# Attention, routing and two networks on one core: weight copies of the routing issued a round earlier, place matrices made on one engine

## The chip, the core and the metric

The kernel runs on one core of a Trainium2 chip. A core has a matrix engine (TensorE, PE in the rows; PEld is its loading of weights), a vector engine (VectorE, DVE), a scalar engine (ScalarE, ACT), a general engine (GpSimd, POOL) and a queue engine (SyncE, SP) that here does nothing but issue transfers (DMAs). Each engine works through its own list of instructions in order, and they wait for each other by semaphores. SBUF is the memory beside the engines, PSUM the one that TensorE writes its products to, and DRAM the large memory. The metric is the time of one execution on the device, in microseconds (us).

## What is computed

Windowed attention, then a mixture of 8 experts in which each token goes to one expert with room for 288 tokens each, then a gated network:

```python
def _moe_ref(x, w_gate, w1, w2):
    N, D = x.shape                      # 2304, 512
    E = w_gate.shape[1]                 # 8
    cap = N // E                        # 288
    logits = x @ w_gate
    order = np.argsort(-logits.flatten())
    ...
    for idx in order:                   # best (token, expert) pair first
        tok, e = (int(idx) // E, int(idx) % E)
        if assigned[tok] >= 0 or counts[e] >= cap:
            continue
        assigned[tok] = e
        counts[e] += 1
    ...
    for e in range(E):
        mask = assigned == e
        out[mask] = np.maximum(x[mask] @ w1[e], 0.0) @ w2[e]

def reference(**kwargs):
    attn_out = _attn_ref(...)           # 4 x 8 heads x 576 x 64, window 64
    x = attn_out.transpose(0, 2, 1, 3).reshape(2304, 512)
    x = _moe_ref(x, ...)
    return _moe2_ref(x, ...)            # silu(x @ w_gate) * (x @ w_val) @ w_out
```

## The kernel before

The program has four stages, one behind the other: attention (all heads, leaving the tokens transposed in `xT`), routing (which expert takes which token), the experts, and the gated network. The order of the instructions on each engine is the order in which the code is written; there is no scheduler.

**Routing.** `routing()` finds the assignment in six rounds of a parallel search, `step(it, ...)`. A round goes over the engines like this. DVE makes from the scores `M` and the shifted logits `U` each token's wish: `m`, `below`, `Us`, `u`, `G` (`wants()`). TensorE counts the wishes in 18 small matmuls (`cnt`). DVE compares the counts with the room (`sat`). TensorE spreads the result to all partitions (`low`, `tot`). ACT copies the count of ties (`ties`) and the new window (`cg`) from PSUM. DVE updates the scores (`lt`, `M`), and POOL narrows `U` with `cg` in four instructions (`narrow()`), which the next round's `Us` reads.

**Beside the routing.** Two other pieces of work are interleaved with the rounds.
- *Rows of tokens.* `store_rows(3)` takes three blocks of 128 tokens: TensorE transposes a block into PSUM (`rowps`, three buffers), ACT copies it to SBUF (`row`, six buffers), and SP stores it to DRAM (`xrows`, 256 KB each). Three blocks (rows 0 to 2) stand ahead of the first round, and three more behind each of the first five rounds (`beside`), 18 in all. The experts later gather their tokens from `xrows` by index, so the first gather waits for all 18 stores.
- *Weight tiles.* The experts' weights come as tiles of 128 x 1024 (512 KB) through four buffers `wraw`, and each is split into a coarse part `whi` and a remainder `wlo`, so that products keep float32 precision. `Stream.half()` does half a tile: ACT copies `whi` (L59), DVE subtracts `wlo` (L60). A round has one such half, between the count and `sat`, so that six rounds split three tiles. `half()` first calls `load()`, which issues the next tile's load on SP once a buffer is to be free: the fifth tile's load takes the first tile's buffer and waits for the `wlo` of its second half, in the second round; the sixth tile's waits for the fourth round, and the seventh's for the sixth.

**Places.** Behind the rounds `assign()` ranks the tokens of each expert, and `places()` makes from each token's place two matrices of zeros and ones, in two halves of nine blocks of tokens. `A` has the place's lower 6 bits. `T` has the upper bits, and `B` is `T` times the token's number, in two parts: part 0 times the block (`crow`), on POOL, and part 1 times the partition (`pcol`), on ACT. `indices()` multiplies `A` and `B` on TensorE (`ps_i`), and DVE adds up the indices (`idx`). Every engine then reads a flag that says whether the search has settled and branches around the slow path; the gathers (POOL, `gather()`) and the experts begin.

Of the kernel before, what the change touches and what calls it, by code (L numbers as in the profile page):

```python
# [12 lines left out]
OP = mybir.AluOpType  # L13
# [5 lines left out]
NT = NTOK // 128  # L19


class Stream:
# [24 lines left out]
    def half(self):  # L47

        if self.nsplit == len(self.todo):
            return  # L50
        self.load(self.nsplit + 5)
        key, _ = self.todo[self.nsplit]
        t = self.raws[self.nsplit]
        if key not in self.parts:
            self.parts[key] = [p.tile(list(t.shape), F32R, name=n) for p, n in ((self.hi, "whi"), (self.lo, "wlo"))]
        h, lo = self.parts[key]
        m = t.shape[1] // 2
        sl = (slice(None), slice(self.nhalf * m, self.nhalf * m + m))
        self.nc.scalar.activation(h[sl], t[sl], AF.Copy)  # L59
        self.nc.vector.tensor_tensor(lo[sl], t[sl], h[sl].bitcast(F32), op=OP.subtract)  # L60
        self.nhalf = 1 - self.nhalf
        self.nsplit += not self.nhalf
# [6 lines left out]
class Kernel:  # L69
# [381 lines left out]
    def build(self):  # L451
        nc, tc = self.nc, self.tc
        self.constants()
        self.weights_setup(self.ctx)

        self.big = self.pool("big", 1).tile([128, 4, NTOK], F32, name="big")
        self.xT = self.big[:, :, 0:NTOK]
        self.ffn_stream()
        with ExitStack() as ctx:
            self.attention(ctx)  # L460
        self.st.open(self.ctx, tc)
        self.xg_ctx = ExitStack()
        self.xg_p, self.xg = self.xg_ctx.enter_context(tc.tile_pool(name="xg", bufs=4, side="right")), {}
        with ExitStack() as ctx:
            self.rows_setup(ctx)
            self.store_rows(3)
            def beside(i):
                self.store_rows(3)
                self.convert_move()

            self.routing(ctx, beside)
        self.ffn()
# [111 lines left out]
    def routing(self, ctx, beside=lambda i: None):  # L584


        nc, L = self.nc, self.L
        mm = nc.tensor.matmul
        BIG = 1.0e30

        def pool(name, bufs, space=None):
            kw = {} if space is None else {"space": space}
            return ctx.enter_context(self.tc.tile_pool(name=name, bufs=bufs, **kw))

        rp, r1 = pool("rp", 2), pool("r1", 1)
        self.rps = pool("rps", 1, PS)
        full = [128, NT, NE]
        first, more = 6, 4
        oh = r1.tile(full, BF, name="oh")
        one = r1.tile([1, NE + first + more], F32, name="one")  # L600
        ties, flag = r1.tile([1, NE], F32, name="ties"), r1.tile([1, 1], I32, name="flag")

        halves = slice(0, 11), slice(11, NT)

        def step(it, M, U, sp, G=None):
            bl = self.below[it % 2]
            if G is None:
                G = rp.tile([128, NT, 32], BF, name="G")
                tmp = [rp.tile([128, NT], F32, name="m"), rp.tile(full, F32, name="Us"), rp.tile([128, NT], BF, name="u")]
                list(self.wants(M, U, bl, G, tmp, halves))  # L610
            cnt = self.rps.tile([32, NE + 1], F32, name="cnt")
            for c in range(NT):
                mm(cnt, G[:, c, :], bl[:, c, :], start=c == 0, stop=c == NT - 1)
            if it < first:
                self.st.half()
            nc.vector.tensor_scalar(self.sat[0:32], cnt[:, 0:NE], cnt[:, NE:NE + 1], 0.5 - CAP,
                                    op0=OP.subtract, op1=OP.is_le)
            nc.scalar.activation(ties, cnt[0:1, 0:NE], AF.Copy, accum_out=one[:, NE + it:NE + it + 1])
            low, ps = self.rps.tile([128, NE], F32, name="low"), self.rps.tile([128, 2, NE], F32, name="tot")
            mm(low, self.weights[0], self.sat, start=True, stop=True)  # L620
            for i in range(2):
                mm(ps[:, i, :], self.weights[i + 1], self.sat, start=True, stop=True)
            cg = sp.tile([128, 2, NE], F32, name="cg")
            nc.scalar.activation(cg, ps, AF.Copy)
            lt = rp.tile(full, F32, name="lt")
            M2 = sp.tile(full, F32, name="M")
            for s in halves:
                nc.vector.tensor_tensor(lt[:, s], U[:, s], low[:, None, :].to_broadcast([128, s.stop - s.start, NE]), op=OP.is_lt)
            for s in halves:
                nc.vector.scalar_tensor_tensor(M2[:, s], lt[:, s], -BIG, M[:, s], op0=OP.mult, op1=OP.add)  # L630
            return M2, cg

        def narrow(U, cg, sp):
            U2 = sp.tile(full, F32, name="U")
            for x, y, i, op in ((U2, U, 0, OP.subtract), (U2, U2, 1, OP.mult)):
                for s in halves:
                    nc.gpsimd.tensor_tensor(x[:, s], y[:, s], cg[:, None, i, :].to_broadcast([128, s.stop - s.start, NE]),
                                            op=op)
            return U2

        def assign(M, n):

            m = rp.tile([128, NT], F32, name="m")
            for s in halves:
                nc.vector.tensor_reduce(m[:, s], M[:, s], axis=AX.X, op=OP.max)
            for s in halves:
                nc.vector.tensor_tensor(oh[:, s], M[:, s], m[:, s, None].to_broadcast([128, s.stop - s.start, NE]), op=OP.is_ge)
            rank = self.ranks(rp, oh)
            tot = self.rps.tile([128, NE], F32, name="tot")
            for c in range(NT):  # L650
                mm(tot, self.onesb, oh[:, c, :], start=c == 0, stop=c == NT - 1)
            off = rp.tile([1, NE + n], F32, name="off")
            wrong = rp.tile([1, 2], F32, name="wrong")
            nc.scalar.activation(off[:, 0:NE], tot[0:1], AF.Square, bias=self.expect[:, 0:1], accum_out=wrong[:, 0:1])
            nc.scalar.activation(off[:, NE:], one[:, NE:NE + n], AF.Square, bias=self.expect[:, 1:2],
                                 accum_out=wrong[:, 1:2])
            self.places(rp, oh, rank)
            nc.vector.tensor_scalar(flag, wrong[:, 0:1], wrong[:, 1:2], 1.0e6, op0=OP.add, op1=OP.min)
            self.indices(rp)

        def unsettled():
            return nc.values_load(flag[0:1, 0:1], min_val=0, max_val=10 ** 6) > 0

        list(self.wants_first(12, NT))
        M, U = L, self.U
        for it in range(first):
            M, cg = step(it, M, U, rp, self.G if it == 0 else None)
            if it < first - 1:
                U = narrow(U, cg, rp)
            beside(it)  # L670
        self.store_rows(NT)
        assign(M, first)
        self.gather_first()
        with self.tc.If(unsettled()), ExitStack() as c1:  # L674
            rq = c1.enter_context(self.tc.tile_pool(name="rq", bufs=2))
            for it in range(first, first + more):
                U = narrow(U, cg, rq)
                M, cg = step(it, M, U, rq)
            assign(M, first + more)
            with self.tc.If(unsettled()), ExitStack() as c2:  # L680
                self.choose(c2, rp)
            self.gather_first()
# [22 lines left out]
    def places(self, rp, oh, rank):  # L705

        nc = self.nc
# [13 lines left out]
        self.B = rp.tile([128, NT, 2, 2 * NT], BF, name="B")  # L721
        T = rp.tile([128, NT, 2 * NT], F32, name="T")
        sq = [128, NT // 2, 2 * NT]
        for s in parts:
            nc.vector.tensor_tensor(T[:, s], self.half[:, None, :].to_broadcast(sq), pt[:, s, None].to_broadcast(sq),
                                    op=OP.is_equal)
        for s in parts:
            nc.gpsimd.tensor_tensor(self.B[:, s, 0, :], T[:, s], self.crow[:, s, None].to_broadcast(sq), op=OP.mult)
            nc.scalar.activation(self.B[:, s, 1, :], T[:, s], AF.Copy, scale=self.pcol)
        for s in parts:  # L730
            sh = [128, NT // 2, 64]
            nc.vector.tensor_tensor(self.A[:, s], self.row[:, None, 0:64].to_broadcast(sh),
                                    pp[:, s, None].to_broadcast(sh), op=OP.is_equal)

# [421 lines left out]
```

## Time and profile before

| | |
|---|---|
| time of the runs | 838.07 us median of 3 (836.49 to 838.79) |
| the profiled execution's own time | 837.96 us |
| its span in the trace | 836.2 us |
| TensorE | busy 803.2 us, 96% of the span |
| DVE | busy 516.7 us, 62% |
| ACT | busy 396.4 us, 47% |
| POOL | busy 95.4 us, 11% |

The span is from the first to the last instruction of the program; a little lies around it. Shares are means over stages with different limits, so a change in one stage is read from that stage. In a row of the timeline the first number is the start of the instruction, the second its duration (of several merged ones, from the first's start to the last's end); in brackets stands how long the engine had been idle and whose end it had waited for.

### The profile page before, as it was taken

How to read it: one execution, taken by the hardware profiler on the slowest of the kernel's cores; microseconds unless marked ns; L12 is line 12 of the kernel's file. 1: busy time of each engine (PE TensorE's matmuls, PEld its weight loads, DVE VectorE, ACT ScalarE, POOL GpSimd, SP SyncE). 2: the span in 40 equal slices, each digit the busy share in tenths (PEclk: the TensorE clock that was granted, in tenths of full speed). 3: DMA queues.
4: the chain of work that ended last, by engine and by line, in shares of the span. 5: the costliest groups of instructions: out<-in, count | busy, mean ns of one | idle time of the engine just before them, and what ended most of it. 6: DMA issues, size and time to landing. Idle time of an engine off the chain costs nothing.

```text
span 836.2 us, 14893 instructions
## 1 busy us (share of the span) xinstructions
PE 803.2 (96%) x5635; PEld 752.7 (90%) x5635; DVE 516.7 (62%) x1104; ACT 396.4 (47%) x998; POOL 95.4 (11%) x167
## 2 busy tenths in 40 slices
PE   8999986499999999999999999999999999999997
PEld 6888966399999999999999999999999999999996
DVE  6777868668888788898774443554453355344322
ACT  5989965346565666674332332333232243222211
POOL 6333323400010000000000000110000012000002
PEclk9999996699999999999999999999999999999999
DMA  8999916569798897777632211331211223220001
GB/s 182 189 192 189 282 49 216 172 192 289 273 294 268 275 287 260 243 265 265 203 115 73 76 51 51 111 116 51 76 51 51 75 89 114 76 67 10 1 1 75
DMA packets 92332, 123.72 MB, mean 148 GB/s; under 512 B 24416, under 2 KB 59232, under 8 KB 92256
## 3 DMA queue, kind: packets, MB, share of 16 engines
q1 hardware_dynamic: 89376, 113.28, 45.9%
q0 software_dynamic: 2880, 9.44, 3.3%
q8 instruction: 46, 0.75, 0.4%
q14 instruction: 30, 0.25, 0.1%
HBM read 99.63 MB, written 18.87 MB: 142 GB/s over the span
## 4 chain that ended last, share of the span: by engine, by line
PE 43%; issue 33%; DVE 2%; POOL 2%; DMA 0%; ACT 0%; POOLq 0%; DVEq 0%; ACTq 0%
PE psw L943 12%; PE psg L943 12%; PE psa L943 11%; PE pso L943 6%; POOL out_dram L1088 1%; PE psw L975 1%; DMA w<-t 0%; DVE wlo L60 0%; PE psw L437 0%; DVE sg L1060 0%; DVE t L896 0%; DVE t L900 0%; ACT xt L935 0%; DVE y L936 0%; POOLq L1152 0%
## 5 line engine op out<-in xcount | busy, mean ns | idle before, releaser
L943 PE MATMUL psg<-y,whi 128*128 128x384 f32 x1152 | 223.1, 336 | 0.0
L943 PEld LDWEIGHTS psg<-y,whi 128*128 128x128 f32 x1152 | 201.6, 188 | 0.0
L60 DVE TENSOR_TENSOR wlo<-wraw,whi 128x512 fp32r<-128x512 f32 x236 | 155.2, 687 | 9.9 <-ACT whi L59 5.2
L59 ACT ACTIVATE whi<-wraw 128x512 fp32r<-128x512 f32 x236 | 136.6, 622 | 2.9 <-ACTq L674 2.9
L1056 DVE TENSOR_TENSOR sg<-sg,psg 128x384 f32<-128x384 f32 x72 | 39.8, 553 | 156.4 <-ACT sg L1055 156.3
L943 PE MATMUL pso<-whi,p 128*128 128x512 f32 x432 | 133.3, 390 | 0.0
L943 PE MATMUL psg<-y,wlo 128*128 128x384 f32 x576 | 123.5, 336 | 0.7 <-DVE sg L1056 0.7
L1055 ACT ACTIVATE sg<-psg 128x384 f32<-128x384 f32 x72 | 35.3, 491 | 174.8 <-PE psg L943 174.8
L943 PEld LDWEIGHTS psg<-y,wlo 128*128 128x128 f32 x576 | 102.5, 188 | 3.8 <-DVE sg L1056 1.2
L1062 ACT ACTIVATE p<-sg 128x384 fp32r<-128x384 f32 x72 | 37.8, 525 | 120.4 <-DVE sg L1060 120.4
L943 PEld LDWEIGHTS pso<-whi,p 128*128 128x128 f32 x432 | 80.6, 188 | 14.5
L943 PE MATMUL pso<-wlo,p 128*128 128x512 f32 x216 | 84.2, 390 | 0.0
L943 PE MATMUL psw<-xt,whi 128*128 128x288 f32 x512 | 78.5, 296 | 0.0
L943 PE MATMUL psa<-hl,whi 128*128 128x288 f32 x256 | 75.6, 295 | 0.1
L943 PE MATMUL psa<-hh,whi 128*128 128x288 f32 x256 | 75.5, 295 | 0.0
L943 PE MATMUL psa<-hh,wlo 128*128 128x288 f32 x256 | 75.3, 294 | 0.0
L943 PEld LDWEIGHTS psw<-xt,whi 128*128 128x128 f32 x512 | 71.5, 188 | 0.0
L1088 POOL DMA_INDIRECT out_dram<-orow,idx x18 | 17.5, 972 | 456.9 <-ACT orow L1086 270.9
L1063 DVE TENSOR_TENSOR p<-sg,p 128x384 fp32r<-128x384 f32 x72 | 40.2, 558 | 42.6 <-ACT p L1062 42.6
L932 ACT ACTIVATE hh<-psw 128x288 fp32r<-128x288 f32 x64 | 26.3, 411 | 58.4 <-PE psw L943 58.4
L226 ACT ACTIVATE pp<-ps_s,nm 128x128 f32<-128x128 f32 x144 | 50.9, 365 | 5.1 <-DVE nm L219 4.5
L1060 DVE TENSOR_TENSOR sg<-sg,psg 128x384 f32<-128x384 f32 x72 | 39.8, 552 | 20.7 <-PE psg L943 20.7
(176 smaller groups left out, 1103.4 us busy)
## 6 DMA issues: line engine op xcount, KB each, us to landing
wraw<-in_moe_w_dram SPq DMA_DIRECT2D x64, 512.0 KB
wraw<-w SPq DMA_DIRECT2D x54, 512.0 KB
w<-t SPq DMA_DIRECT2D x36, 256.0 KB
raw<-in_moe_w_gate_dram SPq DMA_DIRECT2D x12, 512.0 KB
raw<-in_moe_w_val_dram SPq DMA_DIRECT2D x12, 512.0 KB
raw<-in_moe_w_out_dram SPq DMA_DIRECT2D x12, 512.0 KB
rawq<-in_q_dram SPq DMA_DIRECT2D x32, 144.0 KB
rawk<-in_k_dram SPq DMA_DIRECT2D x32, 144.0 KB
```

Source lines behind the costliest of these rows:

```text
L59: self.nc.scalar.activation(h[sl], t[sl], AF.Copy)
L60: self.nc.vector.tensor_tensor(lo[sl], t[sl], h[sl].bitcast(F32), op=OP.subtract)
L226: nc.scalar.activation(PP[g][:, u, :], ps[:, u, :], AF.Exp, bias=nm[:, u:u + 1], scale=scale, accum_out=SM[g][:, u:u + 1])
L932: nc.scalar.activation(h, x, AF.Relu)
L943: self.nc.tensor.matmul(acc, x, y, start=start and i == 0, stop=stop and i == len(seq) - 1)
L975: nc.tensor.transpose(ps[:, d, :], self.xg[t][r0:r1, 128 * d:128 * d + 128], self.ident[r0:r1, r0:r1])
L1055: nc.scalar.activation(sg, pg, AF.Sigmoid)
L1056: nc.vector.tensor_tensor(sg, sg, pg, op=OP.mult)
L1060: nc.vector.tensor_tensor(sg, sg, pv, op=OP.mult)
L1062: nc.scalar.activation(p[0][:, sl], sg, AF.Copy)
L1063: nc.vector.tensor_tensor(p[1][:, sl], sg, p[0][:, sl].bitcast(F32), op=OP.subtract)
L1088: d = nc.gpsimd.indirect_dma_start(out=self.out, out_offset=bass.IndirectOffsetOnAxis(ap=self.idx[:, 6 * g + t:6 * g + t + 1], axis=0), in ...
```

## The change

Two edits.

`half()` is cut in two: `high()` is the ACT copy with what stands ahead of it, the call of `load()` included, and `low()` the DVE subtraction. In the routing `low()` stays where `half()` was. `high()` moves ahead: the first one before the first three rows, and each further one behind `narrow()`, before the row copies of its round. Everywhere else `half()` calls both, one after the other, as before.

In `places()` DVE makes part 0 of `B` in place of POOL, and it does `T`, `B` and `A` of the first half before those of the second.

```diff
     def half(self):
         if self.nsplit == len(self.todo):
             return
+        self.high()
+        self.low()
+
+    def high(self):
         self.load(self.nsplit + 5)
         key, _ = self.todo[self.nsplit]
...
         self.nc.scalar.activation(h[sl], t[sl], AF.Copy)
+        self.next = h, lo, t, sl
+
+    def low(self):
+        h, lo, t, sl = self.next
         self.nc.vector.tensor_tensor(lo[sl], t[sl], h[sl].bitcast(F32), op=OP.subtract)
...
             self.rows_setup(ctx)
+            self.st.high()
             self.store_rows(3)
...
             if it < first:
-                self.st.half()
+                self.st.low()
...
             if it < first - 1:
                 U = narrow(U, cg, rp)
+                self.st.high()
             beside(it)
...
+        sh = [128, NT // 2, 64]
         for s in parts:
             nc.vector.tensor_tensor(T[:, s], self.half[:, None, :].to_broadcast(sq), pt[:, s, None].to_broadcast(sq),
                                     op=OP.is_equal)
-        for s in parts:
-            nc.gpsimd.tensor_tensor(self.B[:, s, 0, :], T[:, s], self.crow[:, s, None].to_broadcast(sq), op=OP.mult)
             nc.scalar.activation(self.B[:, s, 1, :], T[:, s], AF.Copy, scale=self.pcol)
-        for s in parts:
-            sh = [128, NT // 2, 64]
+            nc.vector.tensor_tensor(self.B[:, s, 0, :], T[:, s], self.crow[:, s, None].to_broadcast(sq), op=OP.mult)
             nc.vector.tensor_tensor(self.A[:, s], self.row[:, None, 0:64].to_broadcast(sh),
                                     pp[:, s, None].to_broadcast(sh), op=OP.is_equal)
```

The list of ACT from the last copy ahead of the routing (`lt`) to the second round's `cg`, before (an x3 merges three row copies):

```order
L286 ACTIVATE lt<-ps_l 128x512
L429 ACTIVATE row<-rowps 128x4x2x64 x3
L59 ACTIVATE whi<-wraw 128x512
L618 ACTIVATE ties,one<-cnt 1x8
L624 ACTIVATE cg<-tot 128x16
L429 ACTIVATE row<-rowps 128x4x2x64 x3
L59 ACTIVATE whi<-wraw 128x512
L618 ACTIVATE ties,one<-cnt 1x8
L624 ACTIVATE cg<-tot 128x16
```

The same piece with the change, whose lines are numbered eight or nine higher:

```order
L294 ACTIVATE lt<-ps_l 128x512
L63 ACTIVATE whi<-wraw 128x512
L437 ACTIVATE row<-rowps 128x4x2x64 x3
L627 ACTIVATE ties,one<-cnt 1x8
L633 ACTIVATE cg<-tot 128x16
L63 ACTIVATE whi<-wraw 128x512
L437 ACTIVATE row<-rowps 128x4x2x64 x3
L627 ACTIVATE ties,one<-cnt 1x8
L633 ACTIVATE cg<-tot 128x16
```

In each round `whi` and the three row copies have changed places; `ties` and `cg` stand behind both, as before.

The list of SP through the whole routing, before: stores of rows (`xrows`) and loads of weight tiles (`wraw`), up to the flag of the branch:

```order
L431 DMA xrows<-row 128x512 x3
L43 DMA wraw<-in_moe_w_dram 128x4x256
L431 DMA xrows<-row 128x512 x6
L43 DMA wraw<-in_moe_w_dram 128x2x512
L431 DMA xrows<-row 128x512 x6
L43 DMA wraw<-in_moe_w_dram 128x4x256
L431 DMA xrows<-row 128x512 x3
L662 TENSOR_LOAD flag
```

The same with the change:

```order
L43 DMA wraw<-in_moe_w_dram 128x4x256
L439 DMA xrows<-row 128x512 x6
L43 DMA wraw<-in_moe_w_dram 128x2x512
L439 DMA xrows<-row 128x512 x6
L43 DMA wraw<-in_moe_w_dram 128x4x256
L439 DMA xrows<-row 128x512 x6
L671 TENSOR_LOAD flag
```

Each of the three loads has moved ahead of three stores: 3, 6, 6 and 3 stores around them have become 0, 6, 6 and 6.

The list of DVE in `places()`, from the bits of the place (`pt`, `pp`) to the indices, before:

```order
L718 TENSOR_SCALAR pt<-pos 128x18
L719 TENSOR_SCALAR pp<-pos 128x18
L725 TENSOR_TENSOR T<-half,pt 128x324 x2
L732 TENSOR_TENSOR A<-row,pp 128x576 x2
L658 TENSOR_SCALAR flag<-wrong 1x1
L744 TENSOR_REDUCE idx<-ps_i 64x18 x2
```

With the change:

```order
L728 TENSOR_SCALAR pt<-pos 128x18
L729 TENSOR_SCALAR pp<-pos 128x18
L736 TENSOR_TENSOR T<-half,pt 128x324
L739 TENSOR_TENSOR B<-T,crow 128x9x36
L740 TENSOR_TENSOR A<-row,pp 128x576
L736 TENSOR_TENSOR T<-half,pt 128x324
L739 TENSOR_TENSOR B<-T,crow 128x9x36
L740 TENSOR_TENSOR A<-row,pp 128x576
L667 TENSOR_SCALAR flag<-wrong 1x1
L752 TENSOR_REDUCE idx<-ps_i 64x18 x2
```

DVE has two instructions more, and the order is by halves; POOL, whose list isn't shown, has two fewer.

## Rows read from the trace of the kernel before

**Rows 1.** Stretches: us, busy PE, PEld, DVE, ACT, POOL; PE clock, DMA share, GB/s

```profile
122.20:157.20 35.00, 21.03 (x245) 18.23 (x243) 27.95 (x112) 18.27 (x49) 8.59 (x23) 0.71 0.54 181
166.30:836.20 669.90, 662.92 (x4004) 633.73 (x4004) 395.31 (x694) 273.66 (x546) 31.46 (x49) 1.00 0.42 139
```

**Rows 2.** Waits, 122 to 157: total us, times, longest

```profile
DVE wlo L60 <- ACT whi L59: 3.3, 5, 0.9
```

**Rows 3.** Timeline of the third round: ACT and DVE

```profile
133.88 0.62 ACT L59 ACTIVATE whi<-wraw 128x512 fp32r<-128x512 f32 x1
...
134.53 0.69 DVE L60 TENSOR_TENSOR wlo<-wraw,whi 128x512 fp32r<-128x512 f32 x1 [0.92 <-ACT whi L59]
135.15 0.21 DVE L616 TENSOR_SCALAR sat<-cnt 32x8 bf16<-32x8 f32 x1
...
135.45 0.17 ACT L618 ACTIVATE ties<-cnt 1x8 f32<-1x8 f32 x1 [0.95 <-DVE sat L616]
...
135.72 0.18 ACT L624 ACTIVATE cg<-tot 128x16 f32<-128x16 f32 x1
```

**Rows 4.** Timeline of the SP queue in the routing

```profile
123.59 1.33 SPq L431 DMA_DIRECT2D xrows<-row  x3
130.22 0.38 SPq L43 DMA_DIRECT2D wraw<-in_moe_w_dram  x1
130.66 4.80 SPq L431 DMA_DIRECT2D xrows<-row  x6
139.45 0.38 SPq L43 DMA_DIRECT2D wraw<-in_moe_w_dram  x1
...
148.98 0.38 SPq L43 DMA_DIRECT2D wraw<-in_moe_w_dram  x1
```

**Rows 5.** Timeline of ACT: copies of rows 9 to 11, and of row 15

```profile
136.34 1.84 ACT L429 ACTIVATE row<-rowps 128x512 f32<-128x512 f32 x3 [0.43 <-DMA xrows<-row]
...
145.41 0.60 ACT L429 ACTIVATE row<-rowps 128x512 f32<-128x512 f32 x1 [0.81 <-PE rowps L427]
```

**Rows 6.** Stretches behind the loads, columns as in rows 1

```profile
131.00:134.20 3.20, 2.99 (x30) 2.58 (x29) 2.62 (x12) 2.00 (x4) 1.20 (x4) 0.61 0.86 236
...
152.00:154.00 2.00, 0.00 (x0) 0.00 (x0) 1.97 (x6) 1.56 (x6) 1.09 (x2) 0.50 1.07 401
...
155.00:156.00 1.00, 0.55 (x9) 0.40 (x8) 0.76 (x2) 0.00 (x0) 0.03 (x1) 0.50 0.00 0
```

**Rows 7.** Timeline from the fifth round's window to the sixth's split

```profile
144.42 0.18 ACT L624 ACTIVATE cg<-tot 128x16 f32<-128x16 f32 x1
...
145.92 0.48 DVE L570 SCALAR_TENSOR_TENSOR Us<-below,U 128x88 f32<-128x88 bf16 x2 [0.28 <-POOL U L637]
...
148.26 0.69 DVE L60 TENSOR_TENSOR wlo<-wraw,whi 128x512 fp32r<-128x512 f32 x1 [0.85 <-ACT whi L59]
```

**Rows 8.** Timeline of the place matrices on DVE and POOL

```profile
152.33 0.50 DVE L725 TENSOR_TENSOR T<-half,pt 128x324 f32<-128x324 int32 x1
...
152.91 0.92 POOL L728 TENSOR_TENSOR B<-T,crow 128x324 bf16<-128x324 f32 x1 [6.76 <-DVE T L725]
153.15 1.28 DVE L732 TENSOR_TENSOR A<-row,pp 128x576 bf16<-128x576 int32 x1
153.78 1.24 POOL L728 TENSOR_TENSOR B<-T,crow 128x324 bf16<-128x324 f32 x1
...
154.36 1.28 DVE L732 TENSOR_TENSOR A<-row,pp 128x576 bf16<-128x576 int32 x1
```

**Rows 9.** Timeline of first and third gather, TensorE's use, and the gathers' landing

```profile
157.17 1.22 POOL L443 DMA_INDIRECT xg<-xrows,idx  x1 [2.14 <-DVE idx L744]
...
159.94 0.95 POOL L443 DMA_INDIRECT xg<-xrows,idx  x1 [0.30 <-issue]
...
165.08 0.32 PEld L975 LDWEIGHTS psw<-ident,xg 32*128 32x128 f32 x4 [0.17 <-issue]
...
DMA to landing us min/median/max: 3.7/4.7/5.5
```

## Prediction

> **What bounds the kernel now.** I read the stretches first [rows 1]. From 166.30 us to the end of the span TensorE is busy for 662.92 of 669.90 us: the two networks are one stream of matmuls, and whatever moves their start moves the end one for one. In the 35 us of the routing (122.20 to 157.20) TensorE is busy for 21 us only, and VectorE (DVE) for 27.95. Nothing of the networks can start before the routing has its indices, so here a chain of small dependent steps sets the time. The change touches only this stretch.
>
> The waits of the stretch [rows 2] give one entry of the size that matters: DVE waits 3.3 us in 5 of the 6 rounds for `whi`, ScalarE's (ACT's) copy of half a weight tile. One round shows why [rows 3]. ACT reaches `whi` at 133.88 only, since three row copies stand ahead of it. DVE had nothing to do for 0.92 us, starts `wlo` at 134.53, and `sat`, with which the next part of the round begins, stands behind `wlo` on DVE (135.15). From `sat` the round goes on to `cg` on ACT (135.72), to POOL's new `U`, and over DVE's `Us`, `u` and `G` to the next count.
>
> Three times the SP queue stands in this chain's shadow [rows 4]: a load of a weight tile goes out at 130.22, 139.45 and 148.98, each right behind the `wlo` that frees its buffer (148.26 + 0.69 = 148.95 for the last [rows 7]), and everything behind that load on the queue waits with it.
>
> **The first part: the ACT copy a round earlier.** With `high()` in front of the row copies, `whi` is done long before DVE asks for it, in the first round too: ACT has it before its first row copy, where it waits for TensorE anyway. The 3.3 us of idle time [rows 2] go. Count and `sat` follow at once, since in the round shown the count is through before `wlo` is. **Term 1: -3.3 us.** The ACT copies are as many as before and DVE's `wlo` stays at its place.
>
> But `high()` also holds the call that issues the next load, and so the load moves ahead of three row stores on SP: before, stores 0 to 2 went out at 123.59, ahead of the load of 130.22 [rows 4]. Now they stand behind it, and the load waits for `wlo` of the second round. The row copies have six buffers: row 6 writes into the buffer of row 0, and cannot until store 0 has landed. In the new order that is a store queued behind a 512 KB load. The same comes back two rounds on: rows 12 to 14 need stores 6 to 8, which now stand behind the load that waits for the fourth round's `wlo`.
>
> How long from the issue of the load to the landing of the first store behind it (L)? One row shows it: row 9 waited for store 3, the first behind the load of 130.22, and started at 136.34 after 0.43 us of waiting [rows 5], so L = 136.34 - 130.22 = 6.1 us. The bytes alone give a lower end: load and one store are 0.79 MB, and from 131.00 to 134.20 the DMA engines moved 236 GB/s, 0.76 MB [rows 6], so they are through at about 134.3, L = 4.1. The second such batch has an upper end too: row 15, which needs the first store behind the load of 139.45, started at 145.41 with TensorE as its last wait [rows 5], so there L is at most 6.0. I take 6.1 for the first batch, as the row at the same place says, and the middle of 4.1 and 6.0, 5.0, for the second.
>
> The Trainium skill's page "DMA: Bandwidth & Descriptors" (Why a DMA increments its semaphore by 16 and not by 1) has the engines of one DMA finish independently, and only the last of them completes it; row 9's landing, later than the bytes, agrees. By that rule the slowest engine would count in both batches, 6.1 and 6.0, and the sum would be 1.0 us higher than mine.
>
> What a late landing costs, counted from the load's issue: `sat` of that round started 0.10 us before it (`sat` comes 0.62 after the start of `wlo` [rows 3], the load 0.72 after it [rows 4, 7]). A round without waiting takes 0.57 from `sat` to `cg` [rows 3]; then 2.99 from `cg` (144.42) to the time at which DVE would have started `wlo` (148.26 - 0.85 = 147.41 [rows 7]), in a round in which `Us` was already waiting for POOL's `U`, so that `cg` is what counts; then 0.62: 4.18 in all. Undisturbed, the `sat` two rounds on would come at -0.10 + 2 x 4.18 = 8.26. Disturbed, three row copies (1.84 us [rows 5]) start at L, and `ties` and `cg` of the next round stand behind them on ACT: `cg` at L + 1.84 + 0.27 [rows 3], and `sat` 3.61 later, at L + 5.72. Behind ACT wait POOL's `U`, then DVE's `Us` and `G`, and TensorE's next count; TensorE's transposes of the next rows wait for the same copies but have no use for the time. The cost is L + 5.72 - 8.26 = L - 2.54. **Term 2: +3.6 us** (L = 6.1; 1.6 at 4.1). **Term 3: +2.5 us** (L = 5.0; 1.6 to 3.5). Rows 9 to 11 and 15 to 17 wait for the stores just behind, and are reached later; I cost them at nothing.
>
> At the end six row stores instead of three stand behind the load of 148.98. With three, the DMA engines were idle from 155.00 on, 6.0 us after the load's issue [rows 6]; three more of 262 kB at 401 GB/s [rows 6] make it 8.0. The first gather, which reads all rows, came 8.19 after that load (157.17 [rows 9]). So this one is just hidden, and the gathers have 0.4 us to spare: the third goes out at 159.94 and lands 4.7 later, 164.6, and TensorE takes it up at 165.08 [rows 9]. **Term 4: 0**, up to +1.5 if the last store has a tail of 2 us as in row 9.
>
> **The second part: the place matrices.** Before, DVE makes both halves of T, then both of A, while POOL makes its half of B. A takes 1.28 us per half [rows 8], and both end 0.61 us after an instruction of POOL does: 153.15 + 1.28 = 154.43 against 152.91 + 0.92 = 153.83, and 155.64 against 155.02. So I read A as 0.6 us of work and 0.67 of being held up. Now T, B and A follow on DVE, twice: 0.50 + 0.50 (B has T's shape, its nearest row) + 0.61, twice 1.6, from 152.33 to about 155.5. Before, A ended at 155.64. **Term 5: -0.1 us.** Had A needed 1.28 us of itself, two times 2.28 would end at 156.9, 1.2 us later. ACT's half of B is covered by A in either.
>
> The Trainium skill's page "SBUF — State Buffer" (Who interferes with whom) says that a DVE instruction with two SBUF inputs is held up completely by a GpSimd instruction that reads SBUF. The two ends here agree, and by that rule the term is -0.1 and not +1.2.
>
> **The sum.** The profiled execution took 837.96 us (span 836.2, the rest lies around it), 0.1 below the median of the runs, 838.07. -3.3 + 3.6 + 2.5 + 0 - 0.1 = +2.7: 837.96 + 2.7 = 840.7. With every bound at its low end (L = 4.1 twice) it is -0.2, 837.8; at its high end (L = 6.1 and 6.0) +3.7, 841.7.
>
> **The rivals.**
> *The stores never hold the copies up* (the other side): only terms 1 and 5 stay, -3.4, 834.6. It needs stores 0 to 2 to land before ACT wants row 6, some 1.4 us after the load (`cg` at 0.47, the new `whi` of 0.62 and one step). Against it: no row shows a store landing less than 4 us after a load ahead of it. The point at which the change pays is a mean L of 4.2. Chance 0.07.
> *Landings as early as the bytes allow*: L near 4.1 in both, -0.2 to +1, about 838.4. For it: the 6.1 is one row. Chance 0.18.
> *The gathers become the last wait too*: term 4 at up to 1.5 on top of the forecast, 842.2. For it: the margin computed is 0.2 us. Chance 0.09.
> *A is slow by itself*: +1.3 on the forecast, 842.0; against it both ends of rows 8. Chance 0.04.
> *The forecast*, both stalls in place, +1.3 to +3.9: 0.62.
>
> **How the numbers follow.** 0.3% of 838 is 2.5 us, about what a measurement of this kernel can tell from no change. The forecast's case lies around that line: 0.36 above, 0.26 below. Faster: 0.07 and 0.01 of the second rival, 0.08. Same: 0.26 + 0.17 = 0.43. Slower: 0.36 + 0.09 + 0.04 = 0.49. The range leaves out the first rival and the upper part of the last two: 837.7 to 842.4. For the forecast's case alone it is 839.2 to 841.9.
>
> **What would show it.** Right, if in the profile after the wait of `wlo` for `whi` is gone; if the first row copy of the third group and of the fifth (rows 6 and 12) wait for `xrows` stores for some 3 to 5 us each; if `Us` on DVE waits for POOL's `U` in just those two rounds, some 2 to 4 us each instead of 0.3; if A takes about 0.6 to 0.7 us. Wrong, if the row copies wait for TensorE only, as now; if the third gather lands after TensorE is ready for it; or if the stretch from 166.30 on changes its length by more than a few tenths, which nothing here forecasts.

## The result, and the profile after

| | median us | runs | ratio to the kernel before | 95% interval |
|---|---|---|---|---|
| before, same chip | 837.64 | 6 | 1 | |
| with the change | 843.25 (841.53 to 845.68) | 6 | 1.0065 | 1.0050 to 1.0081 |
| with the change, measured again on another chip | 843.88 (842.40 to 846.92) | 6 | 1.0082 | 1.0062 to 1.0101 |

The change makes the kernel slower, by some 5.6 us, where +2.7 was forecast (840.7, range to 842.4). The profiled execution took 844.9 us, with a span of 842.8.

Three moments of the two profiles show where the time goes; they are the last `sat`, the end of the indices, and the first product of the networks (`psw<-xt,wlo`):

| us from the span's start | before | after | difference |
|---|---|---|---|
| `sat` of the sixth round | 148.87 | 150.78 | +1.9 |
| end of `idx` | 156.87 | 158.77 | +1.9 |
| first product | 166.30 | 171.00 | +4.7 |
| end of the span | 836.2 | 842.8 | +6.6 |

Of the first +1.9, 0.4 is older than the change's place (the first `U` starts at 119.59 and 119.99). Then nothing is lost or won in the place matrices, 2.8 between the indices and the first product, and 1.9 behind it. The first two lines are what the forecast spoke of; what the last two add to them, 2.8 and 1.9 us of this execution, it put at zero. The rows of before behind the table, with the experts' first three loads and the second group of products, which are compared below:

```profile
148.87 0.21 DVE L616 TENSOR_SCALAR sat<-cnt 32x8 bf16<-32x8 f32 x1
...
156.48 0.39 DVE L744 TENSOR_REDUCE idx<-ps_i 64x18 int32<-64x36 f32 x2 [0.72 <-PE ps_i L740]
...
161.71 2.77 SPq L43 DMA_DIRECT2D wraw<-in_moe_w_dram  x3
...
166.30 0.76 PE L943 MATMUL psw<-xt,wlo 128*128 128x288 f32 x4 [0.79 <-ACT xt L935]
...
166.90 1.22 PE L943 MATMUL psw<-xt,whi 128*128 128x288 f32 x8
```

The waits of 122 to 164 us after the change (total us, times, longest), answering [rows 2]. DVE's wait for `whi` is gone from the list; ACT's row copies wait twice for stores, and POOL's first gather has waited 12.2 us for something that the list calls "issue":

```profile
POOL xg L451 <- issue: 12.5, 2, 12.2
ACT row L437 <- DMA xrows<-row: 8.4, 2, 4.9
```

The view of the tile `xrows` in the routing names that something. These are the engines that waited for the row stores (us, times):

```profile
  POOL xg L451: 12.2, 1
  ACT row L437: 8.4, 2
```

The timeline after the change, from the second round's `sat` on (start, duration, engine, line; the idle time before it in brackets), answering [rows 3, 4, 5, 7]. The load goes out 0.11 behind `sat`, six stores follow it, and the row copy that needs the first of them starts at 135.54, 6.03 behind the load. The same comes again at 140.86, where it is 4.69 (145.55). Behind the late copies `Us` on DVE waits 3.62 us for POOL:

```profile
129.40 0.21 DVE L625 TENSOR_SCALAR sat<-cnt 32x8 bf16<-32x8 f32 x1
129.51 0.37 SPq L43 DMA_DIRECT2D wraw<-in_moe_w_dram  x1
...
130.07 5.45 SPq L439 DMA_DIRECT2D xrows<-row  x6
...
133.42 0.21 DVE L625 TENSOR_SCALAR sat<-cnt 32x8 bf16<-32x8 f32 x1
...
135.54 1.87 ACT L437 ACTIVATE row<-rowps 128x512 f32<-128x512 f32 x3 [4.93 <-DMA xrows<-row]
...
137.46 0.16 ACT L633 ACTIVATE cg<-tot 128x16 f32<-128x16 f32 x1
...
138.74 0.48 DVE L579 SCALAR_TENSOR_TENSOR Us<-below,U 128x88 f32<-128x88 bf16 x2 [3.62 <-POOL U L646]
...
140.75 0.21 DVE L625 TENSOR_SCALAR sat<-cnt 32x8 bf16<-32x8 f32 x1
140.86 0.38 SPq L43 DMA_DIRECT2D wraw<-in_moe_w_dram  x1
...
144.85 0.21 DVE L625 TENSOR_SCALAR sat<-cnt 32x8 bf16<-32x8 f32 x1
145.55 1.88 ACT L437 ACTIVATE row<-rowps 128x512 f32<-128x512 f32 x3 [3.51 <-DMA xrows<-row]
...
150.78 0.21 DVE L625 TENSOR_SCALAR sat<-cnt 32x8 bf16<-32x8 f32 x1
```

A round without a wait takes 4.0 to 4.1 us (129.40 to 133.42, 140.75 to 144.85). The two rounds to 140.75 take 11.35 and the two to 150.78 take 10.03, instead of about 8.2: the stalls cost 3.15 and 1.8.

The place matrices on DVE, answering [rows 8]: `A` takes 0.75 per half instead of 1.28, with no POOL beside it. The first half, and the indices:

```profile
155.19 0.75 DVE L740 TENSOR_TENSOR A<-row,pp 128x576 bf16<-128x576 int32 x1
...
158.38 0.39 DVE L752 TENSOR_REDUCE idx<-ps_i 64x18 int32<-64x36 f32 x2 [0.73 <-PE ps_i L748]
```

Then the end of the stage, answering [rows 9]. The first gather goes out at 161.19, 2.4 behind the end of the indices (158.77), where it was 0.3 (157.17 against 156.87). The third gather (164.16) is now behind the first three weight loads of the experts (163.66), and TensorE's transposes of the third tile come 5.87 behind it, with 2.5 us of nothing before them. The first two groups of products take 1.33 and 2.12 us, where they took 0.76 and 1.22:

```profile
161.19 1.22 POOL L451 DMA_INDIRECT xg<-xrows,idx  x1 [12.20 <-issue]
...
163.66 2.87 SPq L43 DMA_DIRECT2D wraw<-in_moe_w_dram  x3
...
164.16 0.95 POOL L451 DMA_INDIRECT xg<-xrows,idx  x1 [0.30 <-remote]
...
170.03 0.60 PE L983 MATMUL psw<-ident,xg 32*128 32x32 f32 x4 [2.50 <-issue]
...
171.00 1.33 PE L951 MATMUL psw<-xt,wlo 128*128 128x288 f32 x4 [0.37 <-ACT xt L943]
...
172.12 2.12 PE L951 MATMUL psw<-xt,whi 128*128 128x288 f32 x8
```

The stretches there (columns as in [rows 1]) show why: TensorE's granted clock is 1.00 at 166, falls while TensorE does nothing from 168 to 170, and is 0.50 (1.2 instead of 2.4 GHz) for the first products.

```profile
166.00:168.00 2.00, 1.16 (x8) 0.68 (x7) 0.82 (x2) 1.03 (x2) 1.30 (x2) 1.00 1.06 340
168.00:170.00 2.00, 0.00 (x0) 0.00 (x1) 0.69 (x1) 0.17 (x1) 0.95 (x1) 0.65 0.88 293
170.00:172.00 2.00, 1.60 (x8) 1.50 (x9) 0.29 (x1) 0.28 (x1) 0.00 (x0) 0.50 1.04 387
172.00:174.00 2.00, 2.00 (x10) 1.89 (x8) 0.00 (x0) 0.00 (x0) 0.00 (x0) 0.50 0.67 258
```

### The profile page after: what moved, and what is told of

Read it like the earlier page. It is cut to its first block, busy times and chain, and to the rows that moved or that the text cites. A ratio compares the mean times of both kernels' runs of the same rounds, so it can differ in the third digit from the quotient of the medians.

```text
span 842.8 us, 14893 instructions
## 1 busy us (share of the span) xinstructions
PE 803.8 (95%) x5635; PEld 752.5 (89%) x5635; DVE 515.6 (61%) x1106; ACT 395.4 (47%) x998; POOL 93.2 (11%) x165
## 4 chain that ended last, share of the span: by engine, by line
PE 43%; issue 34%; DVE 2%; POOL 2%; DMA 1%; ACT 1%; POOLq 0%; DVEq 0%; SPq 0%; ACTq 0%
PE psw L951 12%; PE psg L951 12%; PE psa L951 12%; PE pso L951 6%; POOL out_dram L1096 1%; PE psw L983 1%; DMA xrows<-row 1%; DMA xg<-xrows,idx 0%; DVE wlo L68 0%; ACT whi L63 0%; DVE sg L1068 0%; DVE G L586 0%; DVE t L904 0%; POOL U L646 0%; ACT big L1008 0%
```

## The experiments

The change moves three loads ahead of stores. The first two stand before the stalls of terms 2 and 3, the third before the gathers of term 4, so that they can be moved apart. Ratios are to the kernel before on the same chip; 0.001 is 0.84 us.

**The loads back in their place.** The change, with `load()` called beside `low()`, so that SP's order is that of before:

```diff
     def high(self):
-        self.load(self.nsplit + 5)
...
             if it < first:
+                self.st.load(self.st.nsplit + 5)
                 self.st.low()
```

> The change, but with the call that issues the next weight load back at its old place beside DVE's subtraction; only ACT's copies stand a round ahead, and the place matrices are as in the change. Theory Q (the loads that went ahead of the row stores on the SP queue cost it all): both row copies' waits for stores and the late gather are gone and the 3.3 us before wlo stay gone, so about 834 to 835, faster than before by some 3 us. Rival A (ACT's copies in front of the row copies cost the time themselves): still 840 or more. Rival P (the place matrices cost it): between the two, near 841.

Measured: 835.1 us, ratio 0.9965 [0.9951, 0.9979]. Copies a round ahead and places on DVE, without the moved loads, gain 2.9 us. No row copy waits more than 1.0 for a store. The gather goes out behind the indices, the third one 2 us ahead of the loads:

```profile
154.71 1.22 POOL L451 DMA_INDIRECT xg<-xrows,idx  x1 [10.57 <-DVE idx L753]
...
157.48 0.94 POOL L451 DMA_INDIRECT xg<-xrows,idx  x1 [0.30 <-POOLq L685]
...
159.47 2.77 SPq L43 DMA_DIRECT2D wraw<-in_moe_w_dram  x3
...
163.74 0.78 PE L952 MATMUL psw<-xt,wlo 128*128 128x288 f32 x4 [0.79 <-ACT xt L944]
```

**The places alone.** The kernel before with the second edit only.

> The kernel before with the second edit alone: place matrices by DVE, half by half. Theory Q: no change, within 0.5 us of before (838), with A at about 0.75 us and the end of the places where it was. Rival P: 2 us or more slower. Rival A says nothing here.

Measured: 837.98 us, ratio 1.0008 [0.9991, 1.0025]. `A` takes 0.75 us and the gather goes out at 157.13, where it was 157.17: the second edit moves work and no time. So the 2.9 us above belong to the split, as far as the runs can tell.

```profile
153.25 0.75 DVE L730 TENSOR_TENSOR A<-row,pp 128x576 bf16<-128x576 int32 x1
```

**The split alone.** The first edit without the second.

> The first edit alone: ACT's copies and the loads a round ahead, place matrices as before. Theory Q: as the whole change, about 843, with the two waits of row copies for stores and the gathers late. Rival P: close to before, 838 or less. Rival A: as the whole change.

Measured: 843.85 us (840.01 to 846.81), ratio 1.0083 [1.0054, 1.0112], all of the change's loss. The profiled execution was the fastest of the five, 840.01. Its first gather is late too, by 1.5 behind the indices, but its third gather goes out 1.35 ahead of the three loads: the stores were there 9.4 behind the load and not 10.3, and the three loads went out 5.7 behind the indices and not 4.9. The third gather lands after 4.3 us, and the first product keeps the full clock.

```profile
162.97 0.95 POOL L451 DMA_INDIRECT xg<-xrows,idx  x1 [0.30 <-remote]
...
164.32 2.83 SPq L43 DMA_DIRECT2D wraw<-in_moe_w_dram  x3
...
168.36 0.76 PE L953 MATMUL psw<-xt,wlo 128*128 128x288 f32 x4 [0.56 <-DMA wraw<-in_moe_w_dram]
```

**The loads alone.** The kernel before, with only the three loads moved ahead and nothing of the split:

```diff
             self.rows_setup(ctx)
+            self.st.load(5)
             self.store_rows(3)
...
                 U = narrow(U, cg, rp)
+                self.st.load(self.st.nsplit + 5)
```

> The kernel before with nothing but the three loads moved ahead on the SP queue, to the places that they have in the change; ACT's copies stay behind the row copies. Theory Q: slower than the change itself, since whi now stands behind the row copies that wait, 846 to 850, with the same two waits for stores. Rival A: no change, about 838, since ACT's order is as before. Rival P: no change.

Measured: 850.74 us, ratio 1.0148 [1.0115, 1.0180], +12.4. The row copies wait as in the change (9.6 us in two waits), and here `whi` stands behind them on ACT, so that the stall goes through `wlo` as well:

```profile
DVE wlo L60 <- ACT whi L59: 12.3, 6, 5.1
ACT row L429 <- DMA xrows<-row: 9.6, 2, 5.5
```

The moved loads are the loss, then; the copies a round ahead soften it.

**The first two loads ahead, the third in its old place.** Laid on the version with the loads back:

```diff
+            self.st.load(5)
             self.st.high()
...
                 U = narrow(U, cg, rp)
+                self.st.load(min(self.st.nsplit + 5, 6))
```

> The change with only its first two loads ahead of the row stores; the third is back at its old place, so that three stores and not six stand behind it. Theory Q: the waits of rows 6 and 12 for their stores stay, 5 and 3.5 us as in the change, the gathers go out 0.4 us after the indices as before, and the experts' first product is not late beyond that: the kernel of e1_load_back plus the two delays of 3.2 and 1.8 us, about 840 (839 to 841). Rival G (the late gathers are the whole loss and the waits of the row copies are hidden): 835, as e1_load_back.

Measured: 840.7 us, ratio 1.0032 [1.0020, 1.0043]. That is +5.6 (+/- 1.5) on the version with the loads back, where terms 2 and 3 had 6.1. The gather goes out 0.65 behind the indices (157.98), the third one ahead of the loads (163.31):

```profile
158.63 1.22 POOL L451 DMA_INDIRECT xg<-xrows,idx  x1 [10.33 <-DVE idx L755]
...
161.41 0.95 POOL L451 DMA_INDIRECT xg<-xrows,idx  x1 [0.30 <-POOLq L687]
```

**The third load ahead alone.** On the same version:

```diff
                 U = narrow(U, cg, rp)
+                if self.st.nsplit == 2:
+                    self.st.load(7)
```

> The other half: the kernel of e1_load_back with only the third load ahead, so that six stores stand behind it and no row copy waits for a store. Theory Q: no wait of a row copy, the search's rounds as fast as in e1_load_back, the first gather about 2 us after the indices, and the third one landing after TensorE is ready: 2 to 5 us over e1_load_back, 837 to 840, and more scattered than it. Rival W (the waits of the row copies are the whole loss): 835. Together with e5_stalls_only the two parts should add up to the change's 843.

Measured: 838.34 us, ratio 1.0001 [0.9990, 1.0012]: +3.0 (+/- 1.5) on the version with the loads back. The end of the change's stage is there again without its stalls: the gather 2.3 behind the indices (155.32), the loads ahead of the third gather, the transposes 6.1 behind it, and the first product at half clock. The profiled execution is the slowest of the twelve, 842.0 (they run from 836.87): it shows what the swapped order costs at its dearest, and the median loses less.

```profile
157.58 1.22 POOL L451 DMA_INDIRECT xg<-xrows,idx  x1 [12.19 <-issue]
...
160.17 2.87 SPq L43 DMA_DIRECT2D wraw<-in_moe_w_dram  x3
160.66 0.95 POOL L451 DMA_INDIRECT xg<-xrows,idx  x1 [0.30 <-remote]
...
166.73 0.60 PE L986 MATMUL psw<-ident,xg 32*128 32x32 f32 x4 [2.78 <-issue]
167.70 1.33 PE L954 MATMUL psw<-xt,wlo 128*128 128x288 f32 x4 [0.37 <-ACT xt L946]
```

Without the third load the change's parts give 0.9965 + 0.0067 = 1.0032; the third adds 0.0036, together 1.0068, and the change has 1.0065 and 1.0082.

**TensorE kept busy.** What of the 3 us is the half clock? The change, with twelve products without use ahead of the third tile's transposes:

```diff
-        for p in pieces(0):
+        for i, p in enumerate(pieces(0)):
+            if i == 2:
+                self.warm(psw.tile([128, 512], F32, name="psw"), 12)
             transposed(*p)
```

> The change with 12 more idle matmuls on TensorE between the transposes of the second and of the third gathered tile, where it waited for the gather, nothing else. Theory C (about 2 us of the loss is TensorE's lower granted clock after that wait): the clock stays up to the first product, 1 to 2 us less than the change, 841 to 842.5. Rival: the clock makes no difference, 843 to 843.5.

Measured: 844.38 us, ratio 1.0074 [1.0058, 1.0090]. Run once more, beside the change on one chip:

> The change as it is, beside the next two on one chip. 842 to 845 us; its profile should again show the first gather 2 us or more behind the end of the indices, whatever the order of the third gather and the three loads behind it.

> The change with twelve products without use ahead of the third tile's transposes, once more beside the change on one chip. If TensorE's half clock behind its wait is what costs 1 to 2 us: 1 to 2 us less than the change beside it. If the twelve products cost as much as they give back: the same within 0.7 us.

Measured: the change 843.88 us (1.0082), the version with the twelve products 843.19, ratio 1.0061 [1.0044, 1.0078]. In the second profile of the change the first gather was again 2.5 behind the indices, and the third gather (163.36) behind the loads (162.86). With the twelve products the clock is at 1.00 again before the first products, which run at full speed. The stretches of the second run with them:

```profile
170.00:172.00 2.00, 1.74 (x11) 0.73 (x9) 0.15 (x1) 0.22 (x1) 0.28 (x1) 1.00 1.06 384
172.00:174.00 2.00, 1.85 (x14) 1.71 (x14) 0.29 (x1) 0.05 (x1) 0.00 (x0) 1.00 1.00 375
```

But the times differ from the change's by +0.7 and -1.8 us in the two pairs: no gain that the runs can tell from none. The twelve products take 2.75 us themselves. What the clock costs in the median stays open.

For single executions the profiles tell it. From the first product to the end of the span it is 669.8 to 670.1 us in the nine profiles whose first four matmuls of the networks take 0.76 to 0.79 us, both with the twelve products among them. It is 671.4 to 672.2 in the four in which these take 1.33, at half clock: the change twice, the loads alone and the third load alone. So where the half clock is met it costs 1.5 to 2.3 us behind the first product, and the twelve products give that back. But in both of their profiles the search ended later than in the change's two (`sat` of the sixth round at 151.81 and 151.57, against 150.78 and 150.04), and from the indices to the first product it is still 12.2 and 12.6.

**The loads held until the third gather has landed.** The change, with a copy of 32 bytes out of the third gathered tile ahead of the experts' first loads on SP:

```diff
         self.convert_move()
+        nc.sync.dma_start(pool("held", 1).tile([1, 8], F32, name="held"), self.xg[2][0:1, 0:8])
         self.st.split(6)
```

> The change, with SyncE held ahead of the experts' first three loads until the third gather has landed (a 32-byte copy out of the gathered tile stands ahead of them in its queue). Theory D (the three 512 KB loads make the third gather land late, and with it TensorE's wait and its fall to half clock): the third tile's transposes come 4.5 to 5 us behind that gather's issue instead of 5.8, and the kernel takes 1 to 3 us less than the change beside it. Theory E (the gather lands late only because it starts late, the loads do nothing to it): the transposes come as far behind the gather as in the change, and the time is the change's within 1 us. If the loads are needed early, either is hidden by a later wait of TensorE for weights, which the profile would show.

Measured: 839.68 us (838.61 to 841.05), ratio 1.0019 [1.0009, 1.0029], beside 1.0082 for the change on the same chip: 5.3 us less (+/- 1.9), 4.2 by the medians, and more than the 1 to 3 that were expected. The first gather is as late as in the change (161.59, 2.3 behind the end of the indices at 159.29). Now the third gather has only other gathers beside it, TensorE's transposes come 3.5 behind it, and the first product has the full clock:

```profile
164.77 0.95 POOL L451 DMA_INDIRECT xg<-xrows,idx  x1 [0.30 <-remote]
...
168.24 0.40 PE L983 MATMUL psw<-ident,xg 32*128 32x32 f32 x4 [0.76 <-PE psw L983]
169.01 0.79 PE L951 MATMUL psw<-xt,wlo 128*128 128x288 f32 x4 [0.36 <-ACT xt L943]
```

From the end of the indices to the first product it is 9.7 us, against 12.2 in the change, 9.4 before, and 9.7 in the version with the loads back. Over all profiles it is 9.2 to 9.8 in the seven in which the third gather goes out ahead of the three loads, and 12.2 to 13.0 in the six in which it goes out behind them. The landing time of this one gather is in the view of transfers (operation, count, us from issue to landing). First the change, then the change with the loads held:

```profile
xg<-xrows,idx POOLq DMA_INDIRECT x1, 5.8
```

```profile
xg<-xrows,idx POOLq DMA_INDIRECT x1, 3.4
```

Across the profiles it is 5.8 in both of the change and 6.3 with the loads alone, where the loads go out just ahead of it. It is 4.5 before, 4.3 with the loads back and 4.3 in the fastest execution of the split alone, where they go out behind it.

**Both.** The version with the loads back, and the experts' loads held too, as a control.

> The version with the loads back in their old place, and with SyncE held until the third gather has landed. There the first gather goes out 0.6 us behind the end of the indices, the third gather 2 us ahead of the loads, and the tiles are there before TensorE's eight warming products are over, so that holding the loads has nothing to remove: 834 to 836.5 us, as without it. A control: if it is 2 us or more faster, the loads cost something in every version and not only behind late gathers; if 2 us or more slower, holding the loads has a price of its own, and the experiment of the change with it showed less than the whole cost.

Measured: 835.21 us, ratio 0.9964 [0.9951, 0.9977], the same as without holding (0.9965). Holding the loads has no price that the runs can tell (+/- 1.6 us), and nothing to give where the gathers start in time. What it gave back in the change is therefore the cost of the third gather's meeting with the loads.

## Why the prediction was wrong

**The direction** was the one held likeliest, slower, and the two stalls were found where they were forecast. The time lies above the range, since one step, term 4, was costed at nothing and took 3 to 4 us.

**Term 1** (-3.3): right. The wait for `whi` is gone from the list, and the versions with it alone gain 2.9 us.

**Terms 2 and 3** (+3.6 and +2.5): right in mechanism, a little large in size. L was 6.03 and 4.69 where 6.1 and 5.0 stood. The profile shows stalls of 3.15 and 1.8 us; the runs, 5.6 us for the two. The piece of the sum that was off: `cg` to `sat` with the wait takes 3.29 (137.46 to 140.75) instead of 3.61. With term 1 the stalls of the profile make -3.3 + 3.15 + 1.8 = +1.65, and the last `sat` is 1.5 later (1.9 less the 0.4 from ahead of the change's place). The Trainium skill's page "DMA: Bandwidth & Descriptors" (Why a DMA increments its semaphore by 16 and not by 1) had led to 6.1 and 6.0; the first agrees with the 6.03 measured, while the second was 4.69, nearer to the 4.1 of the bytes.

**Term 5** (-0.1): from `sat` to the end of the indices it is 8.00 before and 7.99 after. `A` fell to 0.75 us, so being held up was the right reading of its 1.28, and its own work is 0.14 per half more than the 0.61 forecast. The rule of "SBUF — State Buffer" (Who interferes with whom) in the Trainium skill agrees: no POOL beside it, and 1.28 becomes 0.75.

**Term 4** (0) is the step that failed: "So this one is just hidden, and the gathers have 0.4 us to spare". It failed in three places, one behind the other.

First, the end of the stores was taken from the bytes, 8.0 behind the load. The bytes were through by then: from 158.80 on, 7.9 behind the load, the DMA engines are busy for 6% of the time. But the gather went out 10.3 behind it (150.88 to 161.19), after a tail of some 2.4 us. The stretch of after:

```profile
158.80:161.19 2.39, 0.00 (x0) 0.00 (x0) 0.00 (x0) 2.39 (x5) 0.00 (x0) 0.50 0.06 20
```

The text had a tail of 2 us as its upper bound, with +1.5, and left it out of the term itself, although it had read just such a tail from row 9 and put it into term 2 (L = 6.1, where the bytes gave 4.1).

Second, a late gather was priced by how late it is, less what there was to spare. In fact a gather that is 2 us late costs next to nothing by itself: with the loads held it is just as late, the time from the indices to the first product is 0.3 longer than before, and the runs (1.0019) are no slower than those with the stalls alone (1.0032). The cost comes from what it meets. The experts' three loads go out 4.8 to 4.9 us behind the end of the indices in both kernels (161.71 and 163.66), since they wait for DVE's first `wlo` behind the branch and not for the gathers. Before, the third gather was 1.8 ahead of them, and now it is 0.5 behind. Its landing was taken as a constant, 4.7; with the loads ahead it is 5.8, and without any beside it 3.4.

Third, TensorE had the half clock when that tile came: in the first profile of the change its clock fell to 0.50 while it waited, in the second it had not risen before. The stretch behind the first product became 1.9 longer (671.8 against the 669.9 of [rows 1]), and its 4004 matmuls were busy for 664.81 us instead of 662.92:

```profile
171.00:842.80 671.80, 664.81 (x4004) 635.47 (x4004) 394.89 (x693) 273.68 (x546) 30.58 (x48) 1.00 0.42 138
```
The text named that very thing as a sign of being wrong, and had no rival for it. How much of the 3 us it is in the median could not be told.

In numbers: without the third load moved, the kernel takes 840.7, which is the forecast (closer than the runs can tell, and so in part by chance); 1.0032 x 837.96 = 840.6 says the same by the ratio. The third load adds 3.0 alone, and 2.8 to 4.2 on top of the others. The rival "the gathers become the last wait too" had the late gather, but priced it by its lateness, which costs nothing here; the meeting with the loads was in no rival.

The version that beats both kernels is the change without the move of the loads: 835.1 us, 2.9 less than before and about 8 less than the change.

## What to carry to other kernels

When a step is moved together with a call that issues a transfer, write the queue's order before and after, and follow every transfer behind it to the one who waits for its landing. Where a margin is a few tenths of a microsecond, do not end at "late by so much": look for what stands next on the other queues at a time of its own, since swapping places with it costs more than the delay. Splitting `high()` from `load()` would have kept the gain.

## What was not expected of the hardware

A gather of a 128-row tile landed 3.4 us behind its issue with only other gathers beside it, 4.3 to 4.5 with three 512 KB loads issued 1.4 to 2 us behind it, and 5.7 to 6.3 with the same loads issued 0.5 us ahead of it. What lies between these two orders no run shows.

The last of six 262 kB stores behind a load let the gather go 10.3 us behind the load's issue, with the DMA engines at 6% in the last 2.4 us of it. Over the eight profiles with this order it was 9.4 to 10.5.

Behind a pause of TensorE of 2.5 us, into which it went with its clock at 1.00, the clock was 0.50 for the next products, which took 1.33 and 2.12 us instead of 0.76 and 1.22; in the second profile of the change the clock had not risen at all before them.
